# Batch 3's tail tokens of q and k: transposed by TensorE products instead of a DMA crossbar transfer, with new lists for three engines

## The chip, the cores and the metric

The kernel runs on 1 core of one Trainium2 chip. The metric is the device time of one execution in microseconds (us); lower is better. A time is the median of several executions. The profile comes from one further execution, recorded instruction by instruction.

## What is computed

Two layers in one kernel: attention with a sliding window of 128 tokens and a linear bias for each head, and behind it a channel mix, whose input is the attention's output with the heads laid side by side. There are 8 batches, 8 heads, 576 tokens and 64 channels a head, so the channel mix has 512 channels in and 1024 inside.

```python
scores = scale * np.matmul(q, k.transpose(0, 1, 3, 2))
bias = slopes[:, None, None] * (-np.abs(rel).astype(np.float32))[None, :, :]
mask = (rel >= 0) & (rel < window)          # window = 128
scores = np.where(mask, scores + bias[None], -1000000000.0)
attn = np.exp(scores - max) / (sum + 1e-09)
x = np.matmul(attn, v)                      # heads side by side: (8, 576, 512)
...
xk = mu_k * x + (1.0 - mu_k) * x_prev       # x_prev: x of the token before, zero at the start
xr = mu_r * x + (1.0 - mu_r) * x_prev
k = np.maximum(xk @ w_k, 0.0)
v = k * k @ w_v
r = 1.0 / (1.0 + np.exp(-(xr @ w_r)))
return r * v
```

## The kernel before

Each batch's 576 tokens are four blocks of 128 and a tail of 64. The heads are taken in four pairs `g`. For each batch and pair the steps are: q and k are brought into a layout with channels on the partitions (`qk` or `qx`); `scores` multiplies them (line 796), ACT takes the exponential into `at` (813), DVE multiplies by a mask (819 to 834); `attend` multiplies with v (862), DVE takes the reciprocal of the sums (868) and scales into `xu` (874); `xu` is transposed into `xt`; and `shift` makes the difference `dl` of neighbouring tokens (961) and the two mixes `xk` and `xr` (968). `channel_mix` then works on stretches of tokens: key products (1085), a relu on ACT (1092), its square `kk` (1064 on ACT, 1066 on DVE), receptance products (1103) with a tanh (1110), value products (1119), and `ot`, the product of both (1124), which SP stores (1149). Batch 0 is cut in two parts to start early, and its work differs in details: its copies of q and k for part 2 are made in two halves for each pair, by ACT or DVE (products at 1180, copies at 766), and a few products on zeros (758) keep PE running at the start.

The tail's 64 tokens of q and 64 of k of a batch are loaded together into one tile `ts`, q on partitions 0 to 63 and k on 64 to 127 (`tail_load`, 587), and must come into `tt` with channels on the partitions. There are two `ts` and two `tt` tiles. For batch 0 that is done by 32 small products (1022) and four copies. For batches 1 and 2, `tails_full` (988) does it by four products with the identity, one for each pair, into one PSUM bank, and one DVE copy of 128x512. For the batches in `XTT`, `tail_flip` (693) has SP issue one crossbar transfer from `ts` to `tt` (697) when both loads have landed. From batch 4 on SP also brings q and k into `qx` by eight crossbar transfers a batch (601), from batch 5 on `xu` into `xt` by four (983). `tt` is read by the second score group of each pair only (`HALF1`, `ps<-tt,qk` at 796).

What sets the order: the kernel first makes a node for each step, with its engines, its dependencies and its buffers. `ORDER` gives, for PE, ACT and DVE, the node numbers in the order in which that engine is to take them. Where a step may run on either ACT or DVE (the squares of the first mixes, `SQ`, and the copies of batch 0's to 2's q and k, `QK0` and `QK1`), the list it stands in decides. `Plan.run` walks the lists and emits the instructions, and hands out the buffers and PSUM banks as it goes. The loads on POOL are in program order; the order on SP (stores and crossbar transfers) follows from the plan. An engine takes its instructions strictly in that order, so one that waits holds up all behind it.

The changed line is 375. `n_split` (1060) cuts as many of the last stores in two (1147) as bring the count of transfers issued by SP and ACT to a multiple of eight; the count has a term `len(XTT)`.

```python
    XTT = range(3, B)
...
        t = op(PE, 0.0565 * G, list(tl[b]) + [n_ident], prio + (0,), emit, [hp], [hs])
        g = virtual("tt", [htt])
        c = [op(DVE, dve_t(512), [t, g], prio + (0,), emit_c, (), [hp])]
```

Of the kernel before, what the change touches and what calls it, by code (L numbers as in the profile page):

```python
# [20 lines left out]

ORDER = {
    "PE": [int(x) for x in """
# [15 lines left out]
""".split()],  # L39
    "ACT": [int(x) for x in """  # L40
# [11 lines left out]
""".split()],  # L52
    "DVE": [int(x) for x in """
# [16 lines left out]
""".split()],  # L70
}

# [229 lines left out]
def kernel(  # L302
# [14 lines left out]
    B, H, S, D = q.shape  # L317
# [54 lines left out]
    FT = ()  # L372
    KQ = ACT
    VCUT = True
    XTT = range(3, B)
    MMASK = True
    VDEP = 0
    TCOST = 1.5
# [221 lines left out]
    def flip(b, i, j, g):  # L600
        return dma(SPE, FLIP * RATE, FISSUE, lambda e: nc.sync.dma_start_transpose(
            out=qx_buf[xbh[b].idx][:, i, :, 128 * j:128 * j + 128],
            in_=cb_buf[ch[b].idx][:, i, j].rearrange("p h d -> p (h d)")),
            [g, (cl[b][NF * i + j], FWAIT)], (), [ch[b]], FLAT, True)
# [88 lines left out]
    def tail_flip(b):  # L693
        htt, hs = Hold("tt"), th[b]
        g = plan.add(VIR, 0.0001, 0.0001, [], (0,), None, [htt])
        tth[b], ttg[b] = htt, g
        ttl[b] = [dma(SPE, FLIP * RATE, FISSUE, lambda e: nc.sync.dma_start_transpose(
            out=tt_buf[htt.idx][:, :, 0:2].rearrange("p g t c -> p g (t c)"),
            in_=ts_buf[hs.idx].rearrange("p h d -> p (h d)")),
            [g] + [(x, FWAIT) for x in tl[b]], (), [hs], FLAT, True)]  # L700

    def batch_load(b, what):
# [7 lines left out]
        elif what == "b":  # L710
            th[b], tl[b] = tail_load(b)
            if b in XB:
                xbh[b] = Hold("qx")
                g_ = virtual("qx", [xbh[b]])
                xbl[b] = [flip(b, i, j, g_) for i in range(2) for j in range(NF)]
            if b in XTT:
                tail_flip(b)
# [288 lines left out]
    def tails(b, prio):  # L1006
        htt = Hold("tt")
        hs = th[b]
        if b in XTT:
            plan.follow(last["tt"], ttg[b])  # L1010
# [47 lines left out]

    n_hw = 39 + sum(4 if g in FT else 2 for g in range(2 if PF else 3)) + 8 * len(XB) + len(XTT) + G * len(XO)
    n_split = -n_hw % 8  # L1060
# [379 lines left out]
```

## Time and profile before

| | us |
|---|---|
| median of 3 runs | 227.56 |
| lowest and highest run | 227.03, 228.19 |
| the profiled execution | 227.15 |
| its span, first to last instruction | 225.3 |

The profile names a product by `out<-in`: `ps<-ident,ts` writes PSUM from `ts` and the identity. "x4" is a count; a time in a timeline row is the start, then the duration of the group from its first start to its last end. Products are pipelined: one starts before the one ahead has ended, so the distance between starts is what a product takes of PE, and a row's duration has a drain behind it. PEld is the loading of PE's stationary operand, SPq the issuing of transfers by SP. In a row on waits, `PE ps L1103 <- ACT rl L1092: 0.5, 1, 0.5` says that products of line 1103 stood 0.5 us in all, once, and that ACT's instruction at line 1092 ended it.

### The profile page before, as it was taken

What the parts mean: (1) busy time and instruction counts of PE and PEld (TensorE: products, weight loads), DVE (VectorE), ACT (ScalarE), POOL (GpSimd) and SP (SyncE); (2) the same over time, 40 slices, a digit from 0 to 9 for tenths busy, and PEclk for the clock granted to TensorE, in tenths of its full rate; (3) what the DMA queues carried; (4) which work ended last, traced back from release to release, by engine and by line L of the source; (5) the groups of instructions that cost most, each with busy time, mean ns of one, the idle gap of its engine ahead of it and who ended that gap; (6) DMA issues with size and microseconds to landing.
All of it is one profiled execution on the core that took longest, in us unless ns stands there. A gap on an engine that the chain in (4) does not pass through costs nothing.

```text
span 225.3 us, 6262 instructions
## 1 busy us (share of the span) xinstructions
PE 216.0 (96%) x2474; PEld 125.3 (56%) x2505; DVE 188.9 (84%) x431; ACT 152.6 (68%) x274; POOL 93.6 (42%) x120
## 2 busy tenths in 40 slices
PE   8979889999999999999999999999999999999994
PEld 5646546755666455456755455446664555466442
DVE  6778998997979898999879988969899999784332
ACT  3689999699999976795589751963587631434701
POOL 8983566589980992365658805200000000000000
PEclk9999999999999999999999999999999999999999
DMA  7999999999999999999999999999963144041034
GB/s 131 148 185 205 191 201 172 204 182 161 176 150 193 136 178 139 210 150 156 207 182 178 157 113 181 122 255 171 146 195 32 48 125 102 32 142 49 0 121 158
DMA packets 132012, 33.70 MB, mean 150 GB/s; under 512 B 118792, under 2 KB 128016, under 8 KB 131984
## 3 DMA queue, kind: packets, MB, share of 16 engines
q0 software_dynamic: 96784, 16.52, 103.9%
q1 hardware_dynamic: 34512, 16.46, 38.0%
q8 instruction: 19, 0.31, 0.5%
q10 hardware_dynamic: 688, 0.33, 0.5%
q14 instruction: 9, 0.07, 0.1%
HBM read 33.56 MB, written 9.44 MB: 191 GB/s over the span
## 4 chain that ended last, share of the span: by engine, by line
PE 82%; DVE 6%; ACT 4%; DMA 3%; POOL 2%; issue 2%; POOLq 0%; DVEq 0%
PE ps L1119 27%; PE ps L1085 26%; PE ps L1103 13%; PE ps L862 7%; PE ps L796 6%; DMA qx<-in_k_dram 3%; ACT at L813 2%; PE ps L918 2%; PE ps L1180 1%; DVE xr L968 1%; DVE at L826 1%; POOL qx L562 1%; POOL vs L566 1%; DVE kk L1066 1%; DVE xk L968 1%
## 5 line engine op out<-in xcount | busy, mean ns | idle before, releaser
L1092 ACT ACTIVATE rl<-ps 128x256 bf16<-128x256 f32 (+2 forms) x104 | 45.5, 474 | 38.8 <-PE ps L1085 35.2
L813 ACT ACTIVATE at<-ps 128x1024 bf16<-128x1024 f32 (+2 forms) x68 | 63.5, 994 | 10.9 <-PE ps L796 10.8
L1085 PE MATMUL ps<-xk,wk_sb 128*128 128x256 bf16 (+2 forms) x411 | 69.9, 313 | 0.3
L1119 PE MATMUL ps<-wv_sb,kk 128*128 128x512 bf16 (+2 forms) x282 | 67.0, 373 | 1.1 <-issue 0.3
L1085 PEld LDWEIGHTS <-wk_sb 128*128 128x128 bf16 x416 | 37.9, 98 | 23.9 <-ACT rl L1092 2.3
L1119 PEld LDWEIGHTS <-kk 128*128 128x128 bf16 x296 | 26.7, 98 | 30.4 <-ACT rs L1110 1.3
L834 DVE TENSOR_TENSOR at<-at,mask 128x1024 bf16<-128x1024 bf16 x56 | 37.1, 681 | 3.9 <-ACT at L813 3.7
L1066 DVE TENSOR_TENSOR kk<-rl 128x256 bf16<-128x256 bf16 (+2 forms) x93 | 29.5, 336 | 12.7 <-ACT rl L1092 12.6
L566 POOL DMA_DIRECT2D vs<-in_v_dram x32 | 28.4, 905 | 25.1 <-PE ps L862 22.6
L1103 PE MATMUL ps<-wr_sb,xr 128*128 128x512 bf16 x132 | 34.5, 379 | 1.6 <-ACT rl L1092 0.5
L1110 ACT ACTIVATE rs<-ps 128x512 bf16<-128x512 f32 x36 | 21.9, 618 | 14.1 <-PE ps L1103 12.3
L1124 DVE SCALAR_TENSOR_TENSOR ot<-rs,ps 128x512 f32<-128x512 bf16 (+2 forms) x37 | 24.3, 666 | 6.2 <-PE ps L1119 5.0
L874 DVE TENSOR_TENSOR xu<-ps,rc 128x640 bf16<-128x640 f32 (+2 forms) x36 | 26.3, 738 | 0.4
L968 DVE SCALAR_TENSOR_TENSOR xr<-dl,mu_sb,xt 128x576 bf16<-128x576 bf16 (+1 forms) x32 | 24.5, 775 | 0.0
L968 DVE SCALAR_TENSOR_TENSOR xk<-dl,mu_sb,xt 128x576 bf16<-128x576 bf16 (+1 forms) x32 | 24.3, 779 | 0.2
L862 PEld LDWEIGHTS <-at 128*128 128x128 bf16 x576 | 21.2, 97 | 5.1 <-ACT at L813 0.5
L862 PE MATMUL ps<-vs,at 128*128 128x65 bf16 x512 | 22.1, 193 | 0.1
L1103 PEld LDWEIGHTS <-xr 128*128 128x128 bf16 x144 | 12.7, 97 | 13.6 <-ACT rl L1092 1.1
L597 POOL DMA_DIRECT2D cb<-in_k_dram x20 | 17.8, 946 | 3.2 <-DMA vs<-in_v_dram 3.2
L597 POOL DMA_DIRECT2D cb<-in_q_dram x20 | 17.7, 919 | 2.5 <-PE ps L1180 1.4
L766 ACT COPY qk<-ps 128x512 bf16<-128x512 bf16 (+1 forms) x28 | 14.5, 564 | 1.0 <-PE ps L1180 0.8
L961 DVE TENSOR_TENSOR dl<-xt 128x576 bf16<-128x576 bf16 (+1 forms) x32 | 13.5, 435 | 0.8 <-ACT xt L766 0.6
(81 smaller groups left out, 183.8 us busy)
## 6 DMA issues: line engine op xcount, KB each, us to landing
out_dram<-ot SPq DMA_DIRECT2D x31, 256.0 KB, 5.6
vs<-in_v_dram POOLq DMA_DIRECT2D x32, 128.0 KB, 7.4
cb<-in_q_dram POOLq DMA_DIRECT2D x20, 128.0 KB, 7.1
cb<-in_k_dram POOLq DMA_DIRECT2D x20, 128.0 KB, 10.8
wk_sb<-in_moe_w_k_dram POOLq DMA_DIRECT2D x2, 512.0 KB, 8.2
cb<-in_q_dram POOLq DMA_DIRECT2D x4, 256.0 KB, 10.0
cb<-in_k_dram POOLq DMA_DIRECT2D x4, 256.0 KB, 10.4
wv_sb<-in_moe_w_v_dram POOLq DMA_DIRECT2D x2, 512.0 KB, 11.1
```

Source lines behind the costliest of these rows:

```text
L566: return dma(POOL, 256, issue_t(1024), lambda e: nc.gpsimd.dma_start(out=vs_buf[h.idx][:, j, :, 0:D], in_=v[b, :, 128 * j:128 * j + 128].r ...
L597: return [dma(POOL, 256, issue_t(1024), lambda e, r=r: nc.gpsimd.dma_start(out=cb_buf[h.idx][:, i, r], in_=src[:, :, r]), [g], kind="q") f ...
L813: lambda e, ah=ah, w=w, hp=hp: nc.scalar.activation(out=ah(), in_=two(hp)[:, :, 0:w], func=AF.Exp, scale=float(scale)), (), [hp])
L834: nc.vector.tensor_tensor(out=a, in0=a, in1=m, op=ALU.mult)
L862: nc.tensor.matmul(a[:, hl, t - t0], lhsT=at[:, lo:lo + 128], rhs=vs[:, u, 2 * g + hl, 0:W] if u < NF else tvb[:, 2 * g + hl, 0:W], start= ...
L874: nc.vector.tensor_tensor(out=out_, in0=a5()[:, :, :, 0:D], in1=rc[:, :, 0:nt, None].to_broadcast([128, 2, nt, D]), op=ALU.mult)
L968: lambda e: nc.vector.scalar_tensor_tensor(out=buf[hk.idx][:, g, e0 + c0:e0 + c1], in0=dls(), scalar=mu[:, g:g + 1], in1=xc(1), op0=ALU.mu ...
L1066: nc.vector.tensor_tensor(out=out, in0=in_, in1=in_, op=ALU.mult)
L1085: nc.tensor.matmul(one(hp)[:, 0:n], lhsT=wk_sb[:, po, 128 * fo:128 * fo + 128], rhs=xk_buf[hx.idx][:, po, c0:c1], start=(po == 0), stop=(p ...
L1092: a = op(ACT, act_t(n), [s], pr, lambda e, hp=hp, hr=hr: nc.scalar.activation(out=rl_buf[hr.idx][:, 0:n], in_=one(hp)[:, 0:n], func=AF.Rel ...
L1103: nc.tensor.matmul(one(hp), lhsT=xr_buf[hx.idx][:, po, 128 * c:128 * c + 128], rhs=wr_sb[:, po], start=(po == 0), stop=(po == NPO - 1))
L1119: nc.tensor.matmul(one(hv)[:, a:b], lhsT=kk_buf[hk.idx][:, fo, o:o + 128], rhs=wv_sb[:, fo, a:b], start=(fo == 0), stop=(fo == NFO - 1))
```

## The change

Batch 3 leaves `XTT`, so its tail is transposed as that of batches 1 and 2: four products by `tails_full` and a DVE copy in place of the transfer at 697. That adds one PE node and one DVE node, so the node numbers behind them shift, and all three lists are new. With one transfer fewer `n_split` goes from 4 to 5.

```diff
 ORDER = {
     "PE": [int(x) for x in """
-49 66 72 54 65 68 63 47 53 60 61 70 40 62 73 59 64 75 50 46 83 81 95 119 97 84 98 69 44 56 121 35 122 107 48 45
...
+44 71 65 43 69 58 50 55 63 48 72 60 40 46 62 64 61 75 70 53 81 95 97 73 119 107 98 83 52 84 109 121 35 122 110
...
@@ -372,7 +372,7 @@
     KQ = ACT
     VCUT = True
-    XTT = range(3, B)
+    XTT = range(4, B)
     MMASK = True
```

On PE, the place of the new products: before, behind the attention products of batch 2's pair 1 (`at`, `tv`), come a key group, a value group and a key group, and then the first score group of batch 3's pair 1 (`qk`). Each row pair is written once here; in the program a key or value group has four of them, a score group's half four.

```order
L862 MATMUL ps_123<-tv0_65,at1_78 128x65
L1085 LDWEIGHTS wk_sb_116
L1085 MATMUL ps_123<-xk0_93,wk_sb_116 128x256
L1119 LDWEIGHTS kk2_102
L1119 MATMUL ps_123<-wv_sb_117,kk2_102 128x512
L796 LDWEIGHTS qk2_73
L796 MATMUL ps_123<-qk2_73 128x256
```

After, at the same place, the value group stands first, then a key group, the four new products (`ts`), two key groups and the scores:

```order
L862 MATMUL ps_123<-tv0_65,at1_78 128x65
L1119 LDWEIGHTS kk2_102
L1119 MATMUL ps_123<-wv_sb_117,kk2_102 128x512
L1085 LDWEIGHTS wk_sb_116
L1085 MATMUL ps_123<-xk0_93,wk_sb_116 128x256
L993 LDWEIGHTS ts1_68
L993 MATMUL ps_123<-ident_112,ts1_68 128x128
L796 LDWEIGHTS qk2_73
L796 MATMUL ps_123<-qk2_73 128x256
```

So the value group has moved ahead of the first key group, and the products on `ts` stand between key groups.

On ACT, from batch 0's first exponentials of part 2 on (`at`), with the copies of q and k (`qk`) and of the attention output (`xt`); before:

```order
L766 COPY qk1_72<-ps_123 128x2x128
L766 COPY xt0_89<-ps_123 128x256
L766 COPY qk3_74<-ps_123 128x2x128 x2
L766 COPY xt0_89<-ps_123 128x256 x3
L766 COPY qk0_71<-ps_123 128x2x128
L813 ACTIVATE at0_77<-ps_123 128x2x384
```

After:

```order
L766 COPY xt0_89<-ps_123 128x256
L766 COPY qk3_74<-ps_123 128x2x128 x2
L766 COPY xt0_89<-ps_123 128x256
L766 COPY qk1_72<-ps_123 128x2x128
L766 COPY xt0_89<-ps_123 128x256
L766 COPY qk1_72<-ps_123 128x2x128
L766 COPY qk0_71<-ps_123 128x2x128
L813 ACTIVATE at0_77<-ps_123 128x2x384
```

One copy to `xt` now stands ahead of all copies of q and k, and both halves of `qk1` are ACT's; one of them was DVE's.

Further on ACT, the relus (`rl`) and squares (`kk`) of the first channel mix ahead of the first copy of part 2's output (`xt`, 128x320); before:

```order
L1092 ACTIVATE rl0_97<-ps_123 128x256
L1092 ACTIVATE rl1_98<-ps_123 128x256
L1092 ACTIVATE rl2_99<-ps_123 128x256
L1064 ACTIVATE kk0_100<-rl0_97 128x256
L1064 ACTIVATE kk0_100<-rl1_98 128x256
L766 COPY xt0_89<-ps_123 128x320 x2
```

After:

```order
L1092 ACTIVATE rl1_98<-ps_123 128x256
L1092 ACTIVATE rl0_97<-ps_123 128x256
L1092 ACTIVATE rl2_99<-ps_123 128x256
L1064 ACTIVATE kk0_100<-rl1_98 128x256
L1064 ACTIVATE kk0_100<-rl2_99 128x256
L1092 ACTIVATE rl1_98<-ps_123 128x256
L1064 ACTIVATE kk0_100<-rl1_98 128x256
L766 COPY xt0_89<-ps_123 128x320
```

One relu of this mix (`rl0`) stands two rows further ahead, in front of the last exponential of batch 0. So five relus and three squares are now ahead of that copy, where three and two were.

On SP, the first stores (`ot`) and crossbar transfers (`qx`, `tt`), as a piece of the difference:

```order
-L1149 DMA out_dram<-ot_107 128x512
+L1149 DMA out_dram<-ot_107 128x512 x3
 L1149 DMA out_dram<-ot_108 128x512
 L1149 DMA out_dram<-ot_107 128x512
-L697 DMA_TRANSPOSE tt_70<-ts_68 128x4x128
+L601 DMA_TRANSPOSE qx_75<-cb_62 128x4x128 x7
 L1149 DMA out_dram<-ot_107 128x512
 L601 DMA_TRANSPOSE qx_75<-cb_62 128x4x128
```

Batch 3's transfer into `tt` is gone, and the stores are handed to other `ot` tiles; seven of batch 4's eight transfers now follow one another behind five stores. The queue of POOL is the same row by row.

82 rows, old and new, of the table ORDER are left out of this document.

## The prediction

> **What bounds the kernel now.** I read the page's head and its chain first, then who waited for whom on PE, then the stages in windows of 8 us (columns: window, PE busy of PE's 8.00, PEld, DVE, ACT, POOL, granted clock, DMA, GB/s), and last the timelines of the stretches where PE has gaps.
>
> ```profile
> span 225.3 us, 6262 instructions
> PE 216.0 (96%) x2474; PEld 125.3 (56%) x2505; DVE 188.9 (84%) x431; ACT 152.6 (68%) x274; POOL 93.6 (42%) x120
> PE 82%; DVE 6%; ACT 4%; DMA 3%; POOL 2%; issue 2%; POOLq 0%; DVEq 0%
> ```
>
> PE is busy for 96% and is 82% of the chain that ended last. A gain must therefore come out of PE's gaps or out of PE's own products, and work added to PE where it has no gap is paid in full.
>
> ```profile
> PE ps L1180 <- DMA qx<-in_k_dram: 1.1, 1, 1.1
> ...
> PE ps L1103 <- ACT rl L1092: 0.5, 1, 0.5
> PE ps L796 <- ACT qk L766: 0.5, 2, 0.3
> ...
> PE ps L1103 <- ACT at L813: 0.3, 1, 0.3
> PE ps L796 <- ACT rs L1110: 0.2, 1, 0.2
> PE ps L796 <- ACT at L813: 0.2, 1, 0.2
> ```
>
> The one wait of PE for a transfer is for batch 0's k at the start. The five rows behind it (0.5+0.5+0.3+0.2+0.2 = 1.7 us) all name ACT. No row names `tt`, `ts` or a crossbar transfer.
>
> ```profile
> 16.00:24.00 8.00, 7.67 (x125) 5.35 (x126) 7.37 (x26) 7.22 (x17) 3.40 (x5) 1.00 1.29 203
> 24.00:32.00 8.00, 6.56 (x185) 3.96 (x184) 7.57 (x21) 7.82 (x20) 5.00 (x7) 1.00 1.46 198
> ...
> 40.00:48.00 8.00, 7.82 (x206) 5.73 (x206) 7.65 (x18) 6.38 (x16) 4.95 (x7) 1.00 1.85 205
> ...
> 64.00:72.00 8.00, 7.68 (x123) 4.83 (x123) 6.36 (x16) 7.41 (x14) 2.60 (x4) 1.00 2.20 163
> ```
>
> So there are two regimes. From the landing of batch 0's data to some 34 us ACT (7.82 of 8) and DVE (7.57) are full and PE is the one that waits. Behind that PE is full and the others have room. The changed place, batch 3's tail at about 69 us, lies in the second regime; the new order of everything else acts in both.
>
> **The change part by part.** *The four products.* Their like is in the trace for batches 1 and 2; batch 1's:
>
> ```profile
> 29.40 0.34 PE L901 MATMUL ps<-ident,xu 128*128 128x128 bf16 x3
> 29.58 0.39 PE L993 MATMUL ps<-ident,ts 128*128 128x128 bf16 x4
> ```
>
> Three products of one shape lead from 29.40 to 29.58, 0.06 us each, so four take 0.24 us of PE. The ends are 0 (PE idles 0.32 us in 64 to 72, and a gap there may swallow them) and 0.39 us (the group with its drain, if nothing overlaps it). I take 0.24, because PE is full there. The trace shows the clock at 1.00 between 40 and 48 us, where the 206 products include batch 2's four of this kind and 40 more transposing products at L918. The Trainium skill ("TensorE: Matmul & The Clock Gate", Part 4: PE-mode transpose) says that transposing products don't count as PE activity for the clock gate, which speaks against this change; the trace does not bear it out for so few among other products, and I carry it as a rival.
>
> *Their inputs and what waits for them.* In the new order the products stand behind a value product and one key product of the channel mix, where the old list has this:
>
> ```profile
> 67.90 1.03 PE L1119 MATMUL ps<-wv_sb,kk 128*128 128x512 bf16 x4
> 68.76 0.60 PE L1085 MATMUL ps<-xk,wk_sb 128*128 128x256 bf16 x4
> 69.30 0.39 PE L796 MATMUL ps<-qk 64*128 64x256 bf16 x4
> 69.52 0.63 PE L918 MATMUL ps<-ident,cb 64*128 64x64 bf16 x32
> ...
> 70.16 0.19 PE L796 MATMUL ps<-tt,qk 64*128 64x64 bf16 x2
> ```
>
> A key group takes about 0.44 us (half of the 0.86 that the value group, twice as wide, takes from 67.90 to 68.76), so the new products start near 69.20. Their input tile must be there by then:
>
> ```profile
> SPq L697 <- DMA ts<-in_k_dram: 3.4, 1, 3.4
> ...
> 58.02 1.30 SPq L697 DMA_TRANSPOSE tt<-ts  x1
> ...
> 65.69 1.27 SPq L601 DMA_TRANSPOSE qx<-cb  x1
> 69.68 0.34 SPq L1149 DMA_DIRECT2D out_dram<-ot  x1
> 70.11 8.01 SPq L601 DMA_TRANSPOSE qx<-cb  x5
> ```
>
> The transfer left at 58.02, as soon as `ts` had landed, so PE finds it 11 us old: no wait. Behind the products comes a DVE copy, whose price batches 1 and 2 show:
>
> ```profile
> L697 SPq DMA_TRANSPOSE tt<-ts x5: 1189/1290/1309, 58.0 to 159.7; - x5
> ...
> L766 DVE COPY tt<-ps x2: 417/421/425, 30.1 to 46.7; 128x512 bf16<-128x512 bf16 x2
> ...
> DMA to landing us min/median/max: 2.4/6.7/7.8
> ```
>
> ```profile
> 68.66 0.28 DVE L1066 TENSOR_TENSOR kk<-rl 128x256 bf16<-128x256 bf16 x1
> 68.96 0.69 DVE L1124 SCALAR_TENSOR_TENSOR ot<-rs,ps 128x512 f32<-128x512 bf16 x1
> ```
>
> DVE has 6.36 busy of 8, so 0.42 us more there costs nothing by itself. But it is a new wait: the second score group of head pair 1 (the 70.16 row), and every product queued behind it on PE, stands until the copy is done. Its slack: the products end at 69.20+0.39 = 69.59. On DVE an `ot` (0.69, from about 68.96) and two squares (0.28 each) stand ahead of the copy, so it runs from about 70.0 to 70.45. Between the four products and the score group PE has two key groups (0.88), half a score group (0.22) and a transposing group (0.47), that is until about 69.20+0.24+1.57 = 71.0. Slack 0.55 us; I take 0, with up to 0.8 (one DVE row of that length more in front) as the other end.
>
> *What goes.* Nobody waits for batch 3's `tt` now (it left at 58.02, landed within 7.8 us at the most, and is read at 70.16), so removing the transfer is worth 0 to the chain. SP loses one issue of 1.3 us. Batch 4's eight crossbar transfers, which began at 65.69 behind four stores, now stand behind five, the fifth being the one of 69.68; then seven go without a store between them. The sixth thus leaves at about 70.1+5x1.3 = 76.6; before, it was the last of the five that ended at 78.12, about as late, and the first product that reads `qx` comes 11 us later (87.81, below): no cost. POOL's queue is unchanged row by row, and batch 3's `ts` tile comes free near 69.6 instead of by 65.8, while batch 5's load into it goes out at 84.28 (below): no cost. One more of the last stores is cut in two, on an SP that has nothing else to do there: no cost.
>
> ```profile
> 87.81 0.39 PE L796 MATMUL ps<-qx 64*128 64x256 bf16 x4
> ...
> 84.28 0.72 POOL L587 DMA_DIRECT2D ts<-in_q_dram  x1
> ```
>
> *The new lists.* The number of key, value, receptance, score and attention products is the same. But ACT has two instructions more and DVE two fewer, apart from the copy: one of the eight copies of q and k for batch 0's second part and one square of the first channel mix change sides, both in the stretch that ACT sets.
>
> ```profile
> 12.93 0.37 ACT L766 COPY qk<-ps 128x256 bf16<-128x256 bf16 x1 [0.77 <-PE ps L1180]
> ...
> 15.39 0.37 ACT L766 COPY qk<-ps 128x256 bf16<-128x256 bf16 x1
> 15.66 0.82 ACT L813 ACTIVATE at<-ps 128x768 bf16<-128x768 f32 x1
> ...
> 25.50 0.45 ACT L1064 ACTIVATE kk<-rl 128x256 bf16<-128x256 bf16 x1
> 25.81 0.96 ACT L1092 ACTIVATE rl<-ps 128x256 bf16<-128x256 f32 x3
> 26.61 0.64 ACT L766 COPY qk<-ps 128x512 bf16<-128x512 bf16 x1
> ```
>
> From start to start the copy is 15.66-15.39 = 0.27 and the square 25.81-25.50 = 0.31: 0.58 us more for ACT. Against it, eight copies stand between ACT's wait for batch 0's k (12.93) and the next exponential (15.66), 0.34 us each; in the new list seven do, the eighth having gone ahead of the wait: 0.34 us earlier. Net 0.24, or 0 where DVE, which loses as much, is the later of the two. I take 0.1, with -0.34 and +0.58 as its ends.
>
> **Sum.** 0.24 + 0.1 = 0.34 us. Against the profiled execution, 227.15 us (its span of 225.3 and 1.85 around it), that is 227.5. That execution lies 0.41 below the median of the three timed runs (227.56); the mean of all four is 227.5, and so I say 227.8.
>
> **The rivals.** *A, faster: the new lists fill PE's gaps.* The 1.7 us for which PE waits for ACT are gaps of order; a list that puts ready products there wins them. Price: -1.7+0.24, so 226.1. For it: five separate waits within 10 us, at a time when PE's later products are long and ready. Against it: ACT's 7.82 of 8, with 0.58 more to do, makes PE wait somewhere in that stretch.
>
> *B, slower: part 1's copies to `xt` come late.* In ACT's new list five relus and three squares of the first mix precede the first copy of batch 0's second part, where three relus and two squares did. Two relus ((26.61-25.81)/3 = 0.27 each) and a square put the chain `xt`, `dl`, `xk` and so the second mix's key products 0.85 us back, and those now stand earlier on PE. With the products (0.24) and the net of ACT (0.24): +1.33, so 228.8. It decides once DVE waits for `xt` there:
>
> ```profile
> 23.72 0.43 ACT L766 COPY xt<-ps 128x320 bf16<-128x320 bf16 x1 [0.33 <-PE ps L901]
> ...
> 25.28 0.32 DVE L961 TENSOR_TENSOR dl<-xt 128x320 bf16<-128x320 bf16 x1
> ```
>
> Now `dl` starts 25.28-24.15 = 1.13 us behind the copy's end, so 0.85 is just covered.
>
> *C, the late copy:* DVE is over 0.55 us late at the new copy and PE stands for batch 3's scores, up to 0.8 us: 228.6 at the most.
>
> *D, the clock:* the four products run at half speed, 0.24 more, 228.0. It is the mechanism of the page named above; nothing in the rows shows it.
>
> **How the numbers follow.** Forecast 0.50, A 0.27, B 0.15, C 0.05, D 0.01, and 0.02 for something worse than B. A measurement of this kernel can tell about 0.5% (1.1 us) from no change. Faster by more: A, 0.27. Slower by more: B at +1.2 just reaches it, and the worse, 0.17. Within: forecast, C and D, 0.56. The range goes from 225.8, a little beyond A, to 229.2, a little beyond B; the forecast's own, from the ends of its terms (0 to 0.39, -0.34 to 0.58, 0 to 0.8), is 227.1 to 229.2.
>
> **What would show it.** Right: four L993 products near 69 us of 0.06 us each, no wait of PE for `ts`, no wait for `tt` at L796, a clock of 1.00 there; one crossbar transfer of `tt` fewer; PE's busy time as before within 0.5 us; PE's waits still mostly for ACT between 24 and 34 us. A shows as these waits shrinking below 0.6 us in all; B as DVE waiting for `xt` near 24 us, and PE for `xk` behind it; C as a wait of L796 for the DVE copy. I am wrong if a new wait of over 1 us stands anywhere behind 40 us, where PE has almost no gaps.

## The result and the profile after

The changed kernel took 228.82 us (median of 20 runs, 227.81 to 230.90) against 227.57 us for the kernel before (20 runs beside them, 227.03 to 229.34): a ratio of 1.0053, 95% interval 1.0033 to 1.0073. The forecast was 227.8 us. From profile to profile it is 228.19 against 227.15 us, +1.04, and the span 226.4 against 225.3; the profiled execution of the changed kernel lies 0.6 us below its median.

The page of the changed kernel, its head (busy time, share of the span, instructions of each engine):

```profile
span 226.4 us, 6266 instructions
PE 216.0 (95%) x2479; PEld 126.0 (56%) x2509; DVE 189.8 (84%) x430; ACT 153.8 (68%) x276; POOL 93.9 (41%) x120
```

PE is busy as long as before (216.0) in a span that is 1.1 us longer, so PE has a new idle stretch. The view of who waited for whom, PE's rows after the change (us in all, times, longest):

```profile
PE ps L1119 <- issue: 1.1, 7, 0.2
...
PE ps L1085 <- DMA wk_sb<-in_moe_w_k_dram: 1.0, 1, 1.0
PE ps L1180 <- issue: 0.8, 1, 0.8
PE ps L1103 <- issue: 0.8, 5, 0.2
PE ps L1180 <- DMA cb<-in_k_dram: 0.4, 1, 0.4
PE ps L862 <- ACT at L813: 0.3, 1, 0.3
...
```

The rows that name ACT fall from 1.7 to 1.0 us in all, and between 24 and 34 us, where PE waited for ACT before, to 0.2. What is new is a wait for a weight load at 18 us, one of 0.4 us for `cb` at 26 us and, of 0.8 us and in one piece, a wait at L1180 for "issue", that is for nothing that the profile shows. The rows of L1119 and L1103 for "issue" are no waits: they consist of pieces of 0.16 us, each ahead of a group of three products where the program has four. Two weight loads lie there back to back and the next product starts 0.22 us behind the second, so what is missing is the record of a product and not its time. The windows of the changed kernel, with the columns used in the prediction, say which one matters:

```profile
16.00:24.00 8.00, 7.04 (x130) 5.09 (x128) 7.39 (x27) 6.81 (x17) 3.02 (x5) 1.00 1.30 203
24.00:32.00 8.00, 7.23 (x151) 4.30 (x149) 7.33 (x20) 7.97 (x20) 5.55 (x7) 1.00 1.45 197
40.00:48.00 8.00, 6.92 (x210) 5.19 (x209) 7.61 (x18) 6.31 (x17) 5.49 (x8) 1.00 1.96 194
64.00:72.00 8.00, 7.68 (x128) 5.14 (x129) 7.09 (x17) 7.48 (x15) 2.62 (x4) 1.00 1.81 152
```

In the first two PE loses 0.63 and wins 0.67 against before: what the wait for `wk_sb` takes is won back in the waits for ACT. In 40 to 48 us PE falls from 7.82 to 6.92, and nothing behind gives that back. At the changed place, 64 to 72, PE is busy for 7.68 as before.

The timelines of PE there, first of the kernel before, then of the changed one (start, duration of the group, idle time ahead of it):

```profile
44.88 1.02 PE L1180 MATMUL ps<-ident,cb 64*64 64x64 bf16 x64
```

```profile
44.82 0.54 PE L1180 MATMUL ps<-ident,cb 64*64 64x64 bf16 x43
46.16 0.62 PE L1180 MATMUL ps<-ident,cb 64*64 64x64 bf16 x53 [0.80 <-issue]
```

These are the 64x64 transposes of batch 2's q and k (`qk_quad`, 32 for each pair). Before, two pairs stand together, now three. Without its drain of 0.19 the group of 43 takes 0.35 us, 8 ns a product. Then PE stands for 1.0 us between two products of the same group, and goes on. It isn't a semaphore: the 44th product is the twelfth of its pair, its inputs are those of its neighbours, and no engine ends the wait. At 8 ns a product the 64 of the kernel before should take 0.71 us and took 1.02, so a smaller gap of the same kind was there before: its 16th product of 64 starts 0.27 us behind the 15th.

**What the gap waits for.** Transfers have a queue that carries instructions. The page of the changed kernel, in its part on queues (packets, MB, share):

```profile
q8 instruction: 19, 0.31, 0.6%
```

19 packets of 16 KB in 226 us; PE's program has 2 x 2509 instructions here (a weight load and a product each), that is 264 a packet, and no other engine has so many. (The loads are all on record and 30 of the products are missing, so counts from the program's start go by the loads.) The view of the transfers in windows of 0.1 us places the packet ahead of the gap; before, 42.9 to 43.0 us, and after, 43.7 to 43.8 us:

```profile
q8 instruction: 1, 0.02, 59.0%
```

In the records the packet starts at 42.92 us before and at 43.79 us after, and the gap ends at 45.27 and 46.16: 2.35 and 2.37 us later. The Trainium skill ("Runtime: NRT & Kernel Launch", Instruction fetch mechanics) says that each engine fetches its instructions in blocks of 16 KiB, 256 instructions, by a queue of its own and one block ahead, and that the fetch is hidden by the pace at which instructions are issued. The packets agree with the first; the second doesn't hold here, where products of 8 ns use up a block faster than a queue full of loads brings the next.

So theory 1: *PE ran out of instructions.* Theory 2: the new lists read batch 2's second `cb` load (pair 3's turn has moved ahead of pair 1's) before it has landed. Theory 3: the products, the copy or the missing transfer cost more than their own time.

### The profile page after: what moved, and what is told of

Its sections match the earlier page's. It is cut to its first block, busy times and chain, and to the rows that moved or that the text cites. A ratio compares the mean times of both kernels' runs of the same rounds, so it can differ in the third digit from the quotient of the medians.

```text
span 226.4 us, 6266 instructions
## 1 busy us (share of the span) xinstructions
PE 216.0 (95%) x2479; PEld 126.0 (56%) x2509; DVE 189.8 (84%) x430; ACT 153.8 (68%) x276; POOL 93.9 (41%) x120
## 4 chain that ended last, share of the span: by engine, by line
PE 78%; ACT 9%; POOL 4%; DMA 3%; issue 3%; DVE 0%; DVEq 0%; POOLq 0%
PE ps L1085 26%; PE ps L1119 26%; PE ps L1103 12%; PE ps L862 6%; PE ps L796 5%; DMA wk_sb<-in_moe_w_k_dram 3%; ACT at L813 3%; ACT rl L1092 2%; POOL vs L566 2%; PE ps L918 2%; ACT xt L766 1%; POOL qx L562 1%; ACT qk L766 1%; ACT kk L1064 1%; ACT rs L1110 1%
## 5 line engine op out<-in xcount | busy, mean ns | idle before, releaser
L1092 ACT ACTIVATE rl<-ps 128x256 bf16<-128x256 f32 (+2 forms) x104 | 46.5, 478 | 45.3 <-PE ps L1085 30.3
L1085 PE MATMUL ps<-xk,wk_sb 128*128 128x256 bf16 (+2 forms) x412 | 70.7, 313 | 1.2 <-DMA wk_sb<-in_moe_w_k_dram 1.0
L1119 PE MATMUL ps<-wv_sb,kk 128*128 128x512 bf16 (+2 forms) x281 | 67.0, 373 | 1.6 <-issue 1.1
L813 ACT ACTIVATE at<-ps 128x1024 bf16<-128x1024 f32 (+2 forms) x68 | 64.2, 988 | 4.9 <-PE ps L796 4.8
L1119 PEld LDWEIGHTS <-kk 128*128 128x128 bf16 x296 | 26.5, 98 | 29.4 <-ACT rl L1092 0.7
L1103 PE MATMUL ps<-wr_sb,xr 128*128 128x512 bf16 x133 | 34.2, 379 | 1.1 <-issue 0.8
L1103 PEld LDWEIGHTS <-xr 128*128 128x128 bf16 x144 | 12.9, 98 | 13.9 <-ACT rl L1092 0.6
```

Of the source, the lines that this page charges most:

```text
L813: lambda e, ah=ah, w=w, hp=hp: nc.scalar.activation(out=ah(), in_=two(hp)[:, :, 0:w], func=AF.Exp, scale=float(scale)), (), [hp])
L1085: nc.tensor.matmul(one(hp)[:, 0:n], lhsT=wk_sb[:, po, 128 * fo:128 * fo + 128], rhs=xk_buf[hx.idx][:, po, c0:c1], start=(po == 0), stop=(p ...
L1092: a = op(ACT, act_t(n), [s], pr, lambda e, hp=hp, hr=hr: nc.scalar.activation(out=rl_buf[hr.idx][:, 0:n], in_=one(hp)[:, 0:n], func=AF.Rel ...
L1103: nc.tensor.matmul(one(hp), lhsT=xr_buf[hx.idx][:, po, 128 * c:128 * c + 128], rhs=wr_sb[:, po], start=(po == 0), stop=(po == NPO - 1))
L1119: nc.tensor.matmul(one(hv)[:, a:b], lhsT=kk_buf[hk.idx][:, fo, o:o + 128], rhs=wv_sb[:, fo, a:b], start=(fo == 0), stop=(fo == NFO - 1))
```

## The experiments

In the first two kernels the line numbers are 3 lower than in the kernel before, in the two phase kernels 3 higher; in the two half kernels the products of line 1180 are at 1179.

**The two halves of the change.** `products_alone` takes the lists of before (numbers from 529 on raised by 2), puts the new PE node behind a key group at about 68 us and the copy behind an `ot`; `lists_alone` takes the new lists without the two nodes.

`products_alone` against the kernel before (its lists in the new numbering, and two entries more):

```diff
     "PE": [int(x) for x in """
...
+529
...
     "DVE": [int(x) for x in """
...
+530
...
-    XTT = range(3, B)
+    XTT = range(4, B)
```

`lists_alone` against the changed kernel (its lists renumbered, without these two):

```diff
     "PE": [int(x) for x in """
...
-529
...
     "DVE": [int(x) for x in """
...
-530
...
-    XTT = range(4, B)
+    XTT = range(3, B)
```

> The lists of the kernel before, with only the four products of batch 3's tails and their VectorE copy put in at about 69 us, and the fifth tt transfer left out. Theory 1 (TensorE runs out of fetched instructions at 45 us under the new lists) and theory 2 (the new lists read batch 2's second cb load too early at 45 us) both put the loss into the lists: here only the products' own time is paid, 4 x 0.058 = +0.2 us, 227.8 us, ratio 1.001, and TensorE's gap in the qk transposes at 45 us stays at about 0.3 us as before. Theory 3 (the products, their copy or the missing transfer cost more than their own time): most of the +1.25 us is here, 228.6 to 228.8 us, ratio about 1.005, with a wait at 69 to 72 us.

> The new lists without the two entries of batch 3's tails; the tails of batch 3 go by the transfer again, as before. Theories 1 and 2: the gap of about 1.0 us at 45 to 46 us inside the 64x64 transposes of batch 2 is there as in the changed kernel, and the time is +0.7 to +1.0 us, 228.3 to 228.6 us, ratio 1.003 to 1.0045. Theory 3: 227.6 us, no difference.

Measured, beside 23 runs of before (227.89): `products_alone` 228.57 us, ratio 1.0035 (1.0015 to 1.0056); `lists_alone` 228.23 us, 1.0013 (0.9995 to 1.0032). The gap follows the lists, as theories 1 and 2 have it: with the old lists the pairs' 64 products take 0.86 us, with the new ones the gap is there. PE in `products_alone`, then in `lists_alone`:

```profile
45.15 0.86 PE L1177 MATMUL ps<-ident,cb 64*64 64x64 bf16 x64
```

```profile
45.15 0.54 PE L1177 MATMUL ps<-ident,cb 64*64 64x64 bf16 x43
46.54 0.63 PE L1177 MATMUL ps<-ident,cb 64*64 64x64 bf16 x53 [0.85 <-issue]
```

But the times fit less well: the products cost more than 0.2, nearly the 228.6 us of theory 3, and the lists less than 0.7. For the products the trace has a reason. Put into the old lists they bring a wait of their own, PE and then ACT of `products_alone`:

```profile
71.67 1.03 PE L1100 MATMUL ps<-wr_sb,xr 128*128 128x512 bf16 x4
72.92 0.61 PE L1082 MATMUL ps<-xk,wk_sb 128*128 128x256 bf16 x4 [0.22 <-ACT at L810]
```

```profile
70.16 1.02 ACT L810 ACTIVATE at<-ps 128x1024 bf16<-128x1024 f32 x1 [0.42 <-PE ps L793]
71.08 0.38 ACT L1089 ACTIVATE rl<-ps 128x256 bf16<-128x256 f32 x1
71.34 0.59 ACT L763 COPY qk<-ps 128x512 bf16<-128x512 bf16 x1
71.81 1.05 ACT L810 ACTIVATE at<-ps 128x1024 bf16<-128x1024 f32 x1
```

PE's scores come later, ACT's exponential waits 0.42 us for them, and a key group then waits for the bank that the exponential of 71.81 frees: it starts at 72.92 in place of 72.53 (four receptance products take 0.86), 0.39 us late. Products and wait make 0.6 of the 0.7 us measured. The new lists have no such wait there.

The lists were run again, for their median and a second profile:

> The new lists without batch 3's products once more, since the first run's median (ratio 1.0013) was below what its profile shows (a gap of 0.85 us at 45 us). Theory 1 (TensorE runs out of fetched instructions at 45 us): the gap is there again, 0.8 to 1.2 us, and the time is 0.7 to 1.0 us above before, ratio 1.003 to 1.0045. If the ratio is again under 1.002, some of the gap is won back elsewhere by the new lists, and more of the changed kernel's loss belongs to the products.

227.90 us, ratio 1.0016 (0.9992 to 1.0040), with the gap in place, 0.8 us from start to start:

```profile
44.21 0.54 PE L1180 MATMUL ps<-ident,cb 64*64 64x64 bf16 x43
45.37 0.62 PE L1180 MATMUL ps<-ident,cb 64*64 64x64 bf16 x53 [0.62 <-issue]
```

So the time was missed twice: by their medians the lists cost 0.1 to 0.35 us over before although the gap alone costs 0.5 to 0.9 more than the old one. Executions of one kernel differ by up to 1 us ahead of 40 us (40.33 and 39.38 in the table below are one kernel), above all in how long PE stands for `wk_sb` (nothing in the list of `lists_again`, 1.6 us in that of `lists_alone`), and medians of 12 runs leave 0.4 us open on either side. How the total divides between products and lists is thus not settled by the times; what the traces say of it stands below.

**The borders of the blocks moved.** If PE waits for a block of 256 instructions, then more instructions early in the program move every border. Both phase kernels cut the warm-up products (758, all issued ahead of 17 us) into narrower ones of the same total width, 64 more of them; the lists stay.

```diff
         def emit_warm(e, w=w):
-            nc.tensor.matmul(one(h_wm)[:, 0:w], lhsT=warm, rhs=warm[:, None].to_broadcast(
...
+            k = {512: 8, 256: 2, 128: 1}[w]
+            for c in range(0, w, w // k):
+                nc.tensor.matmul(one(h_wm)[:, c:c + w // k], lhsT=warm, rhs=warm[:, None].to_broadcast(
...
```

> The changed kernel, same lists; only the warm-up products ahead of 17 us are cut into narrower ones of the same total width, so that 64 more products (128 more instructions) are issued before 17 us in the same time. Theory 1: every border between two blocks of 256 fetched instructions falls 64 products earlier in the program. By the start times in the profile of the changed kernel, the block whose end falls at about 45.9 us then holds 128 products that run in 2.7 us, against a fetch of 4.9 to 6.1 us: TensorE's gap leaves the qk transposes (L1180) and stands behind them, in or before the L918 group at 46 us, with 2.1 to 3.4 us instead of 1.0; the time is 229.9 to 231.2 us. Theory 2: the gap stays where it is with 1.0 us, the time is 228.8 us.

> The kernel before, same lists, with the same cut of the warm-up products (64 more products ahead of 17 us, of the same total width). Theory 1: the block that ends at about 45.8 us holds products of 3.1 us against a fetch of 5.5 to 5.7 us: a gap of about 2.4 us behind the qk transposes at 46 us instead of 0.3 us, and the time is about 229.7 us. Theory 2: no gap of over 0.3 us there, 227.6 us.

Measured: `phase_after` 232.09 us, ratio 1.0177 (1.0131 to 1.0222); `phase_before` 231.92 us, 1.0181 (1.0133 to 1.0229). Theory 2 is out: the gap left the transposes. PE in `phase_after`:

```profile
44.98 1.03 PE L1183 MATMUL ps<-ident,cb 64*64 64x64 bf16 x96
45.94 0.53 PE L921 MATMUL ps<-ident,xu 64*128 64x64 bf16 x11
48.85 0.32 PE L921 MATMUL ps<-ident,xu 64*128 64x64 bf16 x9 [2.38 <-issue]
```

All 96 run through, and PE stops behind the eleventh of the next 20, as foretold, for 2.38 us (2.57 from start to start). Counted from the program's start by the loads, the gap stood ahead of the 729th product and now stands ahead of the 857th: 128 products or 256 instructions on, which is the next border. The kernel before, with nothing but these 64 products more, gets gaps of the same kind at two borders, 382 products apart (three blocks less two products):

```profile
28.30 0.21 PE L1183 MATMUL ps<-ident,cb 64*64 64x64 bf16 x1 [0.97 <-issue]
49.48 0.26 PE L921 MATMUL ps<-ident,xu 64*128 64x64 bf16 x6 [1.62 <-issue]
```

Both times are above what was expected. In `phase_after` the clock fell behind the gap. Its windows (the third number from the end is the granted clock):

```profile
48.00:50.00 2.00, 0.99 (x13) 0.63 (x15) 1.31 (x2) 0.80 (x2) 2.00 (x4) 1.00 2.12 207
50.00:52.00 2.00, 2.00 (x7) 0.76 (x6) 0.46 (x1) 2.00 (x5) 2.00 (x3) 0.55 2.44 162
52.00:54.00 2.00, 2.00 (x10) 0.96 (x9) 0.20 (x1) 0.83 (x2) 2.00 (x4) 0.59 2.42 151
54.00:56.00 2.00, 1.84 (x42) 0.86 (x41) 1.97 (x4) 1.01 (x2) 2.00 (x3) 1.00 2.35 149
```

2 x 0.45 + 2 x 0.41 = 1.72 us of PE's time are lost there. With 1.6 us more of gap (2.57 against 0.99) that is 228.8 + 3.3 = 232.1, the time measured. The one of the four executions whose mean clock was 0.999, where the others have 0.993, took 230.23 us, within what theory 1 had expected for the gap alone. In `phase_before` the gap behind the transposes is there, with 1.81 us where about 2.4 were expected; the gap at 28 us (1.16 from start to start) was not foreseen, nor that its clock would fall early:

```profile
12.00:16.00 4.00, 3.20 (x100) 2.51 (x100) 2.76 (x14) 2.64 (x8) 3.32 (x6) 0.78 1.81 185
16.00:20.00 4.00, 4.00 (x89) 2.93 (x81) 2.56 (x11) 3.54 (x8) 2.13 (x4) 0.80 1.24 206
```

**The unchanged kernels again**, for the noise and for second profiles:

> The kernel before, unchanged, as a test of the measurement and a second profile. All theories: ratio 1.000 within 0.002. Theory 1 (TensorE runs out of fetched instructions): the gap in the qk transposes of batch 2 at 45 us lies again at the same instruction (15th product of the second group of 32), its size between 0.2 and 0.6 us, since it is set by how long one 16 KB fetch waits in the DMA queues.

> The changed kernel, unchanged, for a comparison with the other runs of this call. Ratio 1.005 within 0.002 (228.7 to 229.2 us). Theory 1: the gap stands again behind 43 of the 96 transposes, 0.8 to 1.1 us.

`before_again` 227.78 us, ratio 1.0004 (0.9979 to 1.0029); `after_again` 228.78 us, 1.0036 (1.0008 to 1.0064). The gaps stand at the same instructions as in the first profiles, but one is smaller (0.13 us) and one larger (1.20 us) than was expected. All gaps at these borders, from the records: the first product of the block, the start of the 16 KB packet, and the products on either side of the gap. "Block" is from the border to the last product ahead of the gap.

| kernel | border, us | packet behind it | gap ends behind the packet | block | gap |
|---|---|---|---|---|---|
| before | 39.74 | 3.19 | 2.35 | 5.26 | 0.27 |
| before_again | 40.06 | 3.10 | 2.30 | 5.26 | 0.13 |
| products_alone | 40.00 | 3.07 | 2.31 | 5.27 | 0.11 |
| changed | 40.00 | 3.79 | 2.37 | 5.17 | 0.99 |
| after_again | 40.11 | 3.95 | 2.42 | 5.16 | 1.20 |
| lists_alone | 40.33 | 3.88 | 2.34 | 5.16 | 1.05 |
| lists_again | 39.38 | 3.64 | 2.34 | 5.16 | 0.82 |
| copy4_after | 40.02 | 3.32 | 2.40 | 5.02 | 0.70 |
| amp10_after | 41.10 | 3.42 | 2.46 | 5.17 | 0.71 |
| phase_after | 43.32 | 3.21 | 2.31 | 2.95 | 2.57 |
| phase_before, first | 22.55 | 3.36 | 2.39 | 4.59 | 1.16 |
| phase_before, second | 44.53 | 2.65 | 2.29 | 3.13 | 1.81 |

That the gap is the third and fourth column less the fifth follows from how they are taken. What the table shows is that the fourth column hardly changes: over gaps of 0.1 to 2.6 us PE goes on 2.3 to 2.5 us behind the start of the packet, wherever that lies. What varies is how long after the border the packet starts (2.7 to 4.0 us; that it waits behind the loads in the transfer queues is likely, but was not tried) and how fast the block is used up. The three executions with the old lists have gaps of 0.1 to 0.3 us, the six with the new ones 0.7 to 1.2. From the old lists to the new, by the first profiles, the packet starts 0.60 us later and the block is used up 0.09 us sooner.

**Where the microsecond lies.** At the first product behind this border the old and the new lists have the same work behind them, but for four of the short transposes (0.03 us). Counted from the records, in us from the span's start:

| kernel | this product starts at | from there to the end |
|---|---|---|
| before | 45.27 | 180.02 |
| before_again | 45.45 | 180.36 |
| products_alone | 45.38 | 180.78 |
| changed | 46.16 | 180.27 |
| after_again | 46.47 | 180.30 |
| lists_alone | 46.54 | 180.27 |
| lists_again | 45.37 | 180.27 |

So the changed kernel's loss has been made by the end of the gap (0.7 to 1.2 us there, of which the gap is 0.7 to 1.1), and behind it the changed kernel is as fast as before within the scatter of before. It is also as fast there as the new lists without the four products, so their 0.22 us is not lost at the end. In the old lists it is: `products_alone` takes 0.4 to 0.8 us more there, and it reaches this product no later than before.

**Fewer instructions.** `qk_quad` transposes 128 rows at once, 16 products for a pair instead of 32:

```diff
-                for hl, r in ((0, 0), (1, 1), (1, 0), (0, 1)):
-                    rows = slice(64 * r, 64 * r + 64)
-                    nc.tensor.transpose(
-                        one(hp[r]).bitcast(BF16)[64 * hl:64 * hl + 64, 64 * n:64 * n + 64],
-                        buf()[rows, n // nr, 2 * g + hl, n % nr], ident[rows, rows])
+                for hl in range(2):
+                    nc.tensor.transpose(
+                        one(hp[n // nr]).bitcast(BF16)[
+                            64 * hl:64 * hl + 64, 128 * (n % nr):128 * (n % nr) + 128],
+                        buf()[:, n // nr, 2 * g + hl, n % nr], ident)
...
```

The two copies behind the products change with it: each now brings all of q or all of k, where it brought half of both.

> The changed kernel, same lists, but qk_quad does its transposes over all 128 rows (64x128, 16 products for four blocks) in place of 64x64 pieces (32 products): 160 products fewer in the program, about the same TensorE time (16 x 0.028 against 32 x 0.015 us in a group, -0.3 us over the 12 groups). Theory 1: no block of 256 instructions is used up in less than about 6.5 us by the profile's start times, the fetch takes 4.9 to 6.1 us, so the gap of 1.0 us at 45 us goes: 227.5 us, ratio to before 0.9995 to 1.000. Rival (the new lists lose the time by the order of their waits, whatever the instructions): only the 0.3 us goes, 228.5 us, ratio 1.004.

> The kernel before with the same 64x128 transposes in qk_quad. Theory 1: its gap of 0.3 us at 45 us goes and 0.3 us of products, 227.0 us, ratio 0.9975; the changed kernel in the same form is then only 0.2 to 0.5 us slower (the four products). Rival: 227.3 us, and the changed kernel in the same form stays 1.2 us behind it.

`half_after` 229.26 us, ratio 1.0067 (1.0047 to 1.0087); `half_before` 228.35 us, 1.0020 (0.9996 to 1.0045). The times were missed, and the reason is the price of the new products. PE in `half_after`:

```profile
45.48 1.53 PE L1179 MATMUL ps<-ident,cb 128*64 128x128 bf16 x48
46.94 0.47 PE L918 MATMUL ps<-ident,xu 64*128 64x64 bf16 x20
```

The three pairs run through without a gap, which is theory 1's point. But 48 such products take 1.34 us (drain of 0.19 off), 28 ns each, where the old ones take 8 and not 15: 0.45 against 0.26 us a pair of batch 1 or 2. Eight pairs of that size and four of half of it make some 1.9 us more, not 0.3 less. For `half_after` that is 228.78 - 1.20 + 1.9 = 229.5, near what was measured; `half_before` came about 1.1 below the like sum, and why was not followed up. The two lie 0.9 us apart, where theory 1 had 0.2 to 0.5 and the rival 1.2. So taking the gap away did not bring the changed kernel near the kernel before: in the profiles `half_after` has a wait of 0.8 us for `cb` and one of 0.4 us for DVE at about 190 us that `half_before` hasn't.

**The products and the copy, made dearer.** In `amp10_after` batch 3's four products are issued ten times, in `copy4_after` its copy four times:

```diff
-            for g in range(G):
+            for g in list(range(G)) * (10 if b == 3 else 1):
...
+            for _ in range(4 if b == 3 else 1):
+                copy_any(e, tt_buf[htt.idx][:, :, 0:2].rearrange("p g t c -> p g (t c)"),
...
```

> The changed kernel with batch 3's four tail products issued ten times over (40 in place of 4, the same result). If each product is paid in full: 36 x 0.057 = +2.1 us over the changed kernel, 230.8 us, ratio 1.0135 to 1.015; the blocks of 256 instructions behind 69 us last 8 to 10 us against a fetch of 3.3 to 4.7 us, so no new gap by fetching. If the products lie in waits that TensorE has there anyway: under +1 us, below 229.8 us.

> The changed kernel with VectorE's copy of batch 3's tails done four times over. The copies follow each other at 0.34 us, so the last ends about 1.0 us later, at 71.4 us, and the first reader (71.17 us) waits about 0.3 us for it if the slack is as the profile shows (0.7 us): +0.1 to +0.4 us over the changed kernel, 228.9 to 229.2 us. If VectorE has no slack there, +1.0 us, 229.8 us.

`amp10_after` 230.20 us, ratio 1.0114 (1.0082 to 1.0145), 1.4 to 1.8 us over the changed kernel by its two ratios; `copy4_after` 229.00 us, 1.0067 (1.0041 to 1.0093). PE in `amp10_after`, then in `copy4_after`:

```profile
69.93 2.40 PE L993 MATMUL ps<-ident,ts 128*128 128x128 bf16 x40
72.16 1.04 PE L1085 MATMUL ps<-xk,wk_sb 128*128 128x256 bf16 x8
```

```profile
70.58 0.33 PE L796 MATMUL ps<-qk 64*128 64x256 bf16 x4
71.44 0.20 PE L796 MATMUL ps<-tt,qk 64*128 64x64 bf16 x2 [0.53 <-DVE tt L766]
```

40 products take 2.23 us, 0.056 each, with no gap behind them, so a product there is paid nearly in full; the median lies 0.2 to 0.6 us below the full price of 36 products (2.0 us), which the intervals allow. From the product behind the border of 45 us to the end, as in the table above, `amp10_after` takes 182.24 us, 1.97 more than the changed kernel, and `copy4_after` 180.98, 0.7 more. The three extra copies push the copy's end 1.37 us back and PE's reader 0.69 us (it starts 0.17 behind the product group ahead of it in the changed kernel, shown below, and 0.86 here), so the copy has 0.7 us of slack.

**The same instructions, spread.** `defer_after` alters the changed kernel's lists at one place, ACT's to match PE's. PE's, with T for a pair's transposes, xu for the turning of the attention output, R, V, S for receptance, value and score groups:

```diff
-T0 T3 T1 xu R V V ts V S3 T2 V S1 S3 key key key S1 S2 S2 key key key
+T0 R V xu T3 V ts V S3 T2 V S3 key S2 T1 key key S2 key S1 key key S1
```

> The changed kernel with one place altered in its lists: behind the first group of qk transposes of batch 2, a receptance group and a value group (eight products of 0.21 us) come ahead of the second, and the third goes behind the scores of group 3. The same instructions, but the two blocks that end at about 45 and 51 us now hold products of 6.3 and 5.0 us in place of 4.6 and 4.9. Theory 1: the gap of 1.0 us goes (0.3 us at most is left at either border) and the time falls by 0.6 to 1.0 us, to 227.9 to 228.3 us, ratio 1.001 to 1.003. Rival (the lists lose the time elsewhere): a wait of the same size shows up at the moved groups, 228.8 us.

230.09 us, ratio 1.0117 (1.0091 to 1.0144): slower. The gap did go, but PE of `defer_after` now waits for ACT's copies and exponentials, among others here:

```profile
51.15 0.39 PE L796 MATMUL ps<-qk 64*128 64x256 bf16 x3 [0.59 <-ACT qk L766]
...
54.33 0.39 PE L796 MATMUL ps<-qk 64*128 64x256 bf16 x4 [0.36 <-ACT at L813]
```

ACT got its inputs later and in pieces. So the rival was right that waits come up elsewhere, but it had 228.8 us: neither expectation foresaw a kernel 1.3 us slower than the changed one. No version was found that is without the gap and faster than the changed kernel, so that the time comes back with the gap gone is not shown.

## Why the prediction was nearly right, and where it failed

*The four products* came as said. PE, DVE and SP of the changed kernel:

```profile
69.12 0.39 PE L993 MATMUL ps<-ident,ts 128*128 128x128 bf16 x4
69.34 1.04 PE L1085 MATMUL ps<-xk,wk_sb 128*128 128x256 bf16 x8
70.31 0.39 PE L796 MATMUL ps<-qk 64*128 64x256 bf16 x4
...
71.00 0.33 PE L796 MATMUL ps<-qk 64*128 64x256 bf16 x4
71.17 0.19 PE L796 MATMUL ps<-tt,qk 64*128 64x64 bf16 x2
```

```profile
70.01 0.42 DVE L766 COPY tt<-ps 128x512 bf16<-128x512 bf16 x1
```

```profile
69.72 0.33 SPq L1149 DMA_DIRECT2D out_dram<-ot  x1
70.23 11.20 SPq L601 DMA_TRANSPOSE qx<-cb  x7
```

69.34 - 69.12 = 0.22 us (forecast 0.24, start forecast at 69.20, here 69.12), no wait for `ts`, and `amp10_after` shows the price paid by 36 more. *The copy* runs from 70.01 to 70.43 (forecast 70.0 to 70.45) and its reader starts at 71.17 (71.0): slack 0.7 us where 0.55 was reckoned; rival C did not occur. *SP*: seven crossbar transfers without a store between them, behind the store of 69.7, as said, and nobody waits for them. *The clock* stays at 1.00 with the four products: rival D did not occur.

*The new lists*, taken at +0.1, were the step that failed, and not in ACT's part. "The number of key, value, receptance, score and attention products is the same" was made to mean that the lists change only what ACT and DVE have to do ahead of 34 us; behind that, "PE is full". That part came out small: 0.63 lost and 0.67 won in the windows from 16 to 32 us. Rival A's waits for ACT did nearly vanish there, but waits for `wk_sb` and `cb` took their place, so A's gain was not there; B's sign, a wait for `xt` near 24 us and for `xk` behind it, isn't among the rows. That B's time, 228.8, is the measured one is a coincidence. What the step left out is that PE can also wait for its own instructions, and that a new list moves such a wait and changes its size. A block of 256 instructions is used up in 5.17 us where it was 5.26, the fetch of the next takes 6.2 instead of 5.5, and PE stands 0.99 us instead of 0.27. The three groups of 32 transposes that now stand together make the gap easy to see; the block's 0.09 us is little, and most of the difference is the later fetch.

So the sum lacked a term: the lists' +0.1 should have held the gap's 0.72 (1.07 in the second pair of profiles). With 0.22 for the products where they stand that is 0.94, and added to 227.5, as the prediction did, 228.4, against 228.82 and 228.78 measured; some 0.4 us of the medians is in no term. That the measured time still lies in the forecast's own range is luck: its upper end was made of a dearer group of products, more work for ACT and a late copy, and what came is none of these. The condition named for being wrong, a new wait of over 1 us behind 40 us, was all but met, at 0.99 us in this profile and 1.20 in `after_again`. The row that could have warned was in the trace of before: 64 products in 1.02 us, in a window with PE at 7.82 of 8.

Two things stay open. The packet starts 3.1 to 3.2 us behind the border with the old lists and 3.3 to 4.0 with the new ones, which is the greater part of the difference; what it stands behind, and how the lists bring that about, was not tried. And the times of the halves (0.1 to 0.35 for the lists, 0.7 for the products in the old lists) divide the loss otherwise than the traces, by which the lists alone have the whole gap and are no faster behind it than the changed kernel. The wait at 72.9 us accounts for 0.4 of the 0.7; that the lists alone came 0.6 to 0.9 us below the changed kernel's medians is not accounted for, beyond the scatter of up to 1 us ahead of 40 us.

## What to carry to other kernels

Count instructions as well as time: where many short products stand together while the transfer queues are full, find the 16 KB packets of the instruction queue, lay the program's borders of 256 instructions over the timeline (count weight loads, since products can be missing from the records), and see whether each block lasts longer than its successor's fetch (5.4 to 6.4 us at the border of 40 us). A gap inside a run of like products that "issue" ends is the sign of it. It moves with every instruction put in ahead of it, so an edit can cost a microsecond far from where it was made.

## What the runs showed of the hardware

- An instruction fetch, from the border at which the block ahead begins to the first product of the new one, took 4.9 to 6.4 us between 22 and 50 us, 2.3 to 2.5 of them from the start of its packet on.
- 64x64 transposes, issued in turn for the four pairings of a half of the input's partitions with a half of the output's, take 8 ns each (252 ns for 32); those over all 128 rows, issued in turn to the two halves of the output's partitions, take 28 ns.
- In `phase_after` a gap of 2.4 us was followed, 1.4 us behind its end, by some 3.4 us at half the clock (1.72 us lost, at 0.5). The Trainium skill ("TensorE: Matmul & The Clock Gate", Part 1) puts the fall behind an idle window of about 3.4 us; the stretch at half clock has that length here, but no idle stretch as long stands ahead of it. Nor does the length of the gap alone decide it: in `phase_before` a similar fall (0.78 and 0.80 in the windows above) began 1.4 us behind an idle stretch of only 1.1 us at 12 us, while the same stretch in the kernel before, its own later gap of 1.8 us and the gaps of 1.0 to 1.2 us at 46 us left the clock at 1.00.
